# Two matrix products after an attention stage: other token blocks, and W_out decoded at another place

## Chip, cores and metric

One core of one Trainium2 chip. The metric is the device time of one launch in microseconds, lower is better.

## What is computed

A decayed causal attention over 4 x 8 heads of 576 tokens, then two MLP layers on the 2304 rows of width 512 that it gives (hidden width 2048). All in f32.

```python
def _attn_ref(q, k, v, f):                     # q, k, v: 4 x 8 x 576 x 64
    scores = scale * np.matmul(q, k.transpose(0, 1, 3, 2))
    cum = np.cumsum(np.log(np.clip(f, 0.0001, 1.0)), axis=-1)
    scores = np.where(causal, -1e9, scores + cum[:, :, :, None] - cum[:, :, None, :])
    attn = np.exp(scores - np.max(scores, axis=-1, keepdims=True))
    return np.matmul(attn / (np.sum(attn, axis=-1, keepdims=True) + 1e-09), v)
...
x = attn_out.transpose(0, 2, 1, 3).reshape(2304, 512)
h = x @ w_in;  x = np.maximum(0.01 * h, h) @ w_out          # layer 1: w_in 512 x 2048
h = x @ w_in2; x = (h / (1.0 + np.exp(-h))) @ w_out2        # layer 2
```

## The kernel before

**Engines and precision.** TensorE (PE) does all products. An f32 product is three matmuls of rounded parts (high x high, high x low, low x high), so that each operand is first split by a cast on ScalarE (ACT) and a subtraction on VectorE (DVE). The weights come in a wide format and are decoded (`to_f32`: one ACT and three DVE instructions for 128 x 512 values).

**Attention.** Each of the 4 sequences is worked in two halves, queries 0 to 255 and 256 to 575: 8 half-sequences (`sb`) of 8 heads, 64 heads in all, numbered in the order in which they run. A head of an even `sb` gives 256 tokens, one of an odd `sb` 320. Per head: scores on PE (tile `sps`), mask and row minimum on DVE (L688), exp and scaling on ACT and DVE (`sc`), transposes on PE (`tps`), and for each pair of heads the product with v (`av`). `to_ring` splits its result into the tiles `ring`, the input of layer 1.

**Layer 1.** `CHUNKS` (L52) cuts the 2304 tokens into six blocks of 256, 320, 512, 512, 384 and 320. The first product (`hidden`) runs block by block; in each, 16 slices of the hidden width with 12 matmuls, 192 in all (`hps` in the first block, `hpw` in the others). A block can start as soon as all heads that give its tokens are done (`x_ready`); until attention ends it fills PE between the steps of attention. Even blocks lie in the tiles `ring0`, odd ones in `ring1`; `to_ring` waits for a tile until the block two places before it is done. `gate` applies the leaky ReLU (ACT) and stores the result in DRAM (`g1_d`). After attention the second product (`first_values`, `summed`) reads it back in the same six blocks: `gl` loaded through four tiles `ring0`, each with two slices, split into `gs`, and 192 matmuls per block into `acc`. `finish` stores the result (`x1_d`).

**Weights.** `conv_in` decodes W_in. `conv_out` decodes W_out (ACT and DVE, tiles `wst`, `ct`, `wy`) and puts it in DRAM (`wo_d`), 16 slices; `out_weights` fetches it again (`wz`) when the last block of the first product gives its slots back. During the second product `second_weights` decodes and combines the weights of layer 2 on DVE (`f`), spills them (`w2_d`, L1680) and fetches them (`ws`).

**Layer 2.** Seven products in place of eight (`m`, L1333 and L1472), in blocks of 384 columns, then 256. The banks of PSUM alternate between two sets, block by block.

**What sets the order.** The program is written by a planner (`Plan`) that gives every operation a cost, a rank and the names that it waits for, and issues the lowest rank that is ready on each engine; its times decide nothing but the order. On the chip each engine and the DMA queue SP run their list strictly in that order and wait where data is missing.

Of the kernel before, what the change touches and what calls it, by code (L numbers as in the profile page):

```python
# [21 lines left out]
GT_BUFS = 3  # L22
RING_BUFS = 4
WST_BUFS = 2
WY_BUFS = 3
Z_BUFS = 2
U_BUFS = 2
# [21 lines left out]
EDGES = [[0, 128, 256], [0, 107, 214, 320, 448, 576]]  # L49

TURNS = [[[(0, 1)]], [[(0,), (1,)], [(2,), (3, 4)]]]
CHUNKS = ((0, 256), (256, 320), (576, 512), (1088, 512), (1600, 384), (1984, 320))  # L52
SET_A = ("sp", "sp", "sp", "av")
SET_B = ("h", "h", ("acc", 0), ("acc", 1))

# [203 lines left out]
def fused_kernel(ctx, tc, qt, kt, va, vb, ft, w1, wi2, wo2, out):  # L259
# [6 lines left out]
    T = 256  # L266
    TW = 512
    NCH = len(CHUNKS)
    NST = FF // 2
    NP = FF // 2  # L270
    NSB = 2 * B
# [16 lines left out]
    cum_d = dram.tile([H * B, 4, S], F32, name="cum_d")  # L288
    cum_p = dram.tile([H * B, 2, S], F32, name="cum_p")
    wo_d = dram.tile([FF, 128, DM], F32, name="wo_d")  # L290
    g1_d = dram.tile([NCH, NST, 128, 2, TW], F32, name="g1_d")
    x1_d = dram.tile([NG, 128, KC, 2 * TB], F32, name="x1_d")
    g2_d = dram.tile([NG, 4, 128, 4, 2, TB], F32, name="g2_d")
    w2_d = dram.tile([2, 128, 2 * NU, 256], F32, name="w2_d")
# [708 lines left out]
        signal("hidden")  # L1003

    def gate(j, s):
        n = CHUNKS[j][1]
        i_g = yield take("g", G_BUFS)
        if (j, s) == (NCH - 1, NST - 1):
            signal("gated")
        g = main.tile([128, 2, n], F32, tag="g", name="gw", bufs=G_BUFS)  # L1010
        if j == 0:
            hp_t, held = hp.pop((j, 2 * s))
            yield act(2 * n, lambda: nc.scalar.activation(g, hp_t, ACTF.Prelu, alpha=0.01), 1, 0.05)
            give(*held)
        else:
            for part in range(2):
                yield wait(("hp", j, 2 * s + part))
                hp_t, held = hp.pop((j, 2 * s + part))
                yield act(n, lambda: nc.scalar.activation(g[:, part], hp_t, ACTF.Prelu, alpha=0.01), 1, 0.05)
                give(*held)  # L1020
        yield dma(1024 * n, lambda: nc.sync.dma_start(out=g1_d[j, s, :, :, 0:n], in_=g))
        give("g", i_g)
        signal(("g1", j, s))
        if (j, s) == (NCH - 1, NST - 1):
            one = stats[0][0:1, 0:1]
            yield op("act", 1.4, lambda: nc.scalar.activation(one, one, ACTF.Silu), 0)
# [23 lines left out]

    def first_values():

        yield wait(("ring_free", NCH - 2))

        def split(j, s, n, cuts, src, i):
            flat = src.rearrange("p a t -> p (a t)")
            for parts in cuts:
                cols = len(parts) * n
                part = flat[:, parts[0] * n:(parts[-1] + 1) * n]
                i_g = yield take("g", G_BUFS)  # L1060
                t = main.tile([128, 2, cols], F32R, tag="g", name="gs", bufs=G_BUFS)
                yield act(cols, lambda: nc.scalar.copy(t[:, 0], part), 0, 0.09)  # L1062
                yield less(cols, t[:, 1], part, f32(t[:, 0]), "d", 0, PE_LAT)
                for k, a in enumerate(parts):
                    gs[j, 2 * s + a] = t[:, :, k * n:(k + 1) * n], i_g if k == len(parts) - 1 else None
                    signal(("gs", j, 2 * s + a))
            give("ring0", i)

        def splits():
            yield wait("gated")  # L1070
            for j, (_, n) in enumerate(CHUNKS):
                for s in range(NST):
                    yield wait(("gl", j, s))
                    yield from split(j, s, n, ((0, 1),) if j == 0 else ((0,), (1,)), *loaded.pop((j, s)))
            signal("g_last")

        loaded = {}
        p.start(splits())
        for j, (_, n) in enumerate(CHUNKS):
            for s in range(NST):  # L1080
                yield wait(("g1", j, s))
                i = yield take("ring0", RING_BUFS)
                src = main.tile([128, 2, n], F32, tag="ring0", name="gl", bufs=RING_BUFS)
                yield dma(1024 * n, lambda: nc.sync.dma_start(out=src, in_=g1_d[j, s, :, :, 0:n]), 0)
                loaded[j, s] = src, i
                signal(("gl", j, s))

    def summed():
        for j, (_, n) in enumerate(CHUNKS):
            yield wait("hidden" if j else "attention")  # L1090
            acc, held = [], []
            for name in (SET_A, SET_B)[j % 2]:
                t, h = yield from bank(name, [128, n], "acc")
                acc.append(t)
                held.append(h)
            signal(("set", j))
            for f in range(FF):
                yield wait(("gs", j, f), ("woh", f))
                w, i_w = wo_h[f]
                g, i_g = gs.pop((j, f))  # L1100

                def product(c):
                    for r, (wi, gi) in enumerate(((0, 0), (0, 1), (1, 0))):
                        nc.tensor.matmul(  # L1104
                            acc[c], w[:, wi, c * 128:(c + 1) * 128], g[:, gi],
                            start=(f == 0 and r == 0), stop=(f == FF - 1 and r == 2), skip_group_check=True,
                        )

                for c in range(KC):
                    yield op("pe", mm_cost(n, 3), lambda: product(c), 1, 0)  # L1110
                if i_g is not None:
                    give("g", i_g)
                if j == NCH - 1:
                    give(("w", ROOM_W[f]), i_w)
            p.start(finish(j, acc, held))
        signal("summed")

    def finish(j, acc, held):
        o, n = CHUNKS[j]

        def one(c):
            i = yield take("gtmp", GT_BUFS)
# [51 lines left out]
    def second_input():  # L1174
        yield wait("attention")
        for g in range(NG):
            yield wait(*[("x1", j) for j, (o, n) in enumerate(CHUNKS) if o < 2 * TB * (g + 1) and o + n > 2 * TB * g])
            if g:
                yield wait(("m", NP * g - STAGE_LEAD[g - 1], 7))
            i_f = yield take("f", F_BUFS)  # L1180
# [54 lines left out]

    def acc_set():

        k = sets_n[0] % 2
        sets_n[0] += 1
        names = [("sp", 3)] * 3 + [("av", 1)] if k == 0 else [("h", 2)] * 2 + [(("acc", a), 1) for a in range(2)]  # L1240
        held, banks = [], []
        for name, bufs in names:
# [51 lines left out]
    def order2():  # L1294
        items = []
        for n, (g, j) in enumerate(pairs):
            turn = TURN_FIRST[n] if n < 2 else TURN_LAST if n == len(pairs) - 1 else TURN
            items += [(7 * n + pos, n, g, j, q) for q, pos in turn]
        return sorted(items)

    def bank2(n, role):

        name, bufs = ((("sp", 3), ("sp", 3), ("av", 1)), (("h", 2), (("acc", 1), 1), ("h", 2)))[n % 2][role]
        i = yield take(name, bufs)
        pool_, tag = (ps_h, "h") if name == "h" else (ps_acc, f"acc{name[1]}") if name[0] == "acc" else (ps_at, name)
        return pool_.tile([128, TB], F32, tag=tag, name="m", bufs=bufs), (name, i)
# [1 line left out]
    def hidden2():  # L1308
        yield wait("attention")
        held = {}  # L1310
        for _, n, g, j, q in order2():
            if q == 1:
                if n < 2:
                    yield wait(("set", NCH - 2 + n))
                held[n] = [(yield from bank2(n, 0)), None, None]
                p.start(gate2(n, g, j, held[n]))
            if q == 5:
# [274 lines left out]
    def first_weights():  # L1592
# [206 lines left out]
```

## Time and profile before

| | us |
|---|---|
| median of 3 runs | 979.99 (979.06 to 984.43) |
| profiled execution | 978.69 |
| its span | 977.0 |
| PE busy | 961.0 (98%) |
| DVE busy | 678.2 (69%) |
| ACT busy | 573.3 (59%) |

Attention lasts to about 360 us, the first product to 407 us, the second to 617 us, then come the two products of layer 2. A matmul is recorded from its start to the modelled end, and neighbours overlap; what one costs is the distance between starts, so the length of a run divided by its count.

### The profile page before, as it was taken

Reading aid. Unit: us, or ns where it says so; the run is one execution under the profiler, and the core shown is the slowest. Engines: PE = TensorE matmul, PEld = TensorE weight load, DVE = VectorE, ACT = ScalarE, POOL = GpSimd, SP = SyncE. Lnnn points to the kernel's source line nnn. Section 1 sums busy time; section 2 is a strip of 40 time slices with the busy share of each in tenths; the row PEclk is TensorE's granted clock in tenths of the full one; section 3 lists DMA queues with packets and bytes.
Section 4 is the critical chain, followed back from the end, with each engine's and each line's share of the span. In section 5 each row is a group of like instructions: output and inputs, shape, how many; then the busy total and the mean of one; then the engine's idle time right before and its main releaser. Section 6 shows DMA issues by size and latency. Waiting matters only on the chain.

```text
span 977.0 us, 17674 instructions
## 1 busy us (share of the span) xinstructions
PE 961.0 (98%) x6241; PEld 874.6 (90%) x6241; DVE 678.2 (69%) x1673; ACT 573.3 (59%) x1285; POOL 62.6 (6%) x79
## 2 busy tenths in 40 slices
PE   9999999999999999999999999999999999999998
PEld 8787987787677889998788899999999999999998
DVE  6998899798678620478777885434144489998884
ACT  7988898877577633634333444546456665454442
POOL 2001221122112000000000000000000020000000
PEclk9999999999899999999999999999999999999999
DMA  8933676785164215789979878552267764554442
GB/s 234 293 105 122 210 237 204 235 276 167 52 205 143 93 65 172 239 309 330 339 278 344 275 278 252 185 196 101 97 203 220 234 216 131 151 152 132 129 129 65
DMA packets 135252, 190.47 MB, mean 195 GB/s; under 512 B 9958, under 2 KB 105854, under 8 KB 135132
## 3 DMA queue, kind: packets, MB, share of 16 engines
q1 hardware_dynamic: 134732, 188.95, 59.7%
q8 instruction: 49, 0.80, 0.3%
q10 hardware_dynamic: 432, 0.39, 0.1%
q14 instruction: 39, 0.32, 0.1%
HBM read 122.79 MB, written 66.50 MB: 194 GB/s over the span
## 4 chain that ended last, share of the span: by engine, by line
PE 82%; DVE 9%; DMA 4%; ACT 3%; issue 2%; SPq 0%; DVEq 0%; ACTq 0%
PE m L1333 18%; PE m L1472 17%; PE hpw L926 16%; PE acc L1104 13%; PE sps L708 6%; PE av L857 5%; PE tps L789 5%; DMA wst<-in_wi_dram 1%; PE hps L926 1%; DMA wz<-wo_d 1%; PE fps L429 1%; DVE gs L337 1%; DVE sc L688 1%; DMA wst<-in_wo_dram 1%; DVE xa L337 1%
## 5 line engine op out<-in xcount | busy, mean ns | idle before, releaser
L926 PE MATMUL hpw<-ring,w 128*128 128x320 f32 (+2 forms) x960 | 207.3, 353 | 0.3 <-DVE ring L337 0.2
L1104 PE MATMUL acc<-gs,wo 128*128 128x320 f32 (+3 forms) x1152 | 202.6, 336 | 3.6 <-ACT gs L1062 2.1
L1104 PEld LDWEIGHTS acc<-gs,wo 128*128 128x128 f32 x1152 | 185.1, 188 | 20.5 <-DVE gs L337 2.8
L926 PEld LDWEIGHTS hpw<-ring,w 128*128 128x128 f32 x960 | 157.1, 189 | 10.3 <-DVE ring L337 0.9
L1333 PE MATMUL m<-xa,w 128*128 128x384 f32 x576 | 113.5, 339 | 0.6 <-ACT m L1359 0.6
L1472 PE MATMUL m<-w,xa 128*128 128x256 f32 x924 | 113.2, 280 | 0.7 <-DVE xa L337 0.6
L1472 PEld LDWEIGHTS m<-w,xa 128*128 128x128 f32 x924 | 110.6, 188 | 1.4 <-DVE xa L337 1.3
L731 ACT ACTIVATE sc<-sc,st 128x576 f32<-128x576 f32 (+4 forms) x160 | 93.1, 582 | 28.8 <-DVE st L688 27.2
L1333 PEld LDWEIGHTS m<-xa,w 128*128 128x128 f32 x576 | 101.9, 188 | 1.1 <-ACT m L1359 0.9
L1062 ACT CAST gs<-gl 128x512 fp32r<-128x512 f32 (+2 forms) x88 | 47.3, 543 | 84.3 <-PE acc L1104 75.2
L688 DVE CUSTOM_DVE_ANT_0 sc<-sps,zmask 128x288 f32<-128x288 f32 (+4 forms) x160 | 71.3, 449 | 27.7 <-PE sps L708 19.6
L1333 PE MATMUL m<-xb,w 128*128 128x384 f32 x432 | 86.3, 336 | 0.3 <-ACT z L1373 0.3
L322 ACT CAST xa<-g 128x512 fp32r<-128x512 f32 x88 | 49.6, 568 | 48.5 <-PE m L1472 26.0
L1333 PEld LDWEIGHTS m<-xb,w 128*128 128x128 f32 x432 | 76.0, 188 | 0.8 <-ACT z L1373 0.7
L1472 PE MATMUL m<-w,xb 128*128 128x256 f32 x588 | 74.2, 283 | 0.3 <-DVE xb L337 0.3
L789 PE MATMUL tps<-ident,sc 66*107 66x66 f32 (+3 forms) x480 | 68.8, 273 | 5.0 <-ACT sc L741 1.9
L1472 PEld LDWEIGHTS m<-w,xb 128*128 128x128 f32 x588 | 72.0, 191 | 0.7 <-DVE xb L337 0.7
L789 PEld LDWEIGHTS tps<-ident,sc 66*107 66x107 f32 (+3 forms) x480 | 56.0, 152 | 17.5 <-ACT sc L741 3.4
L337 DVE TENSOR_TENSOR gs<-gl,gs 128x512 fp32r<-128x512 f32 (+2 forms) x88 | 51.7, 591 | 28.3 <-ACT gs L1062 28.0
L333 POOL TENSOR_TENSOR m<-qk,m 64x288 fp32r<-64x288 f32 (+1 forms) x58 | 51.9, 905 | 262.9 <-ACT m L322 161.9
L708 PE MATMUL sps<-m,s 66*128 66x288 f32 (+9 forms) x288 | 66.6, 315 | 0.3 <-ACT pf L322 0.2
L1171 DVE TENSOR_TENSOR g<-g 128x256 f32<-128x256 f32 x144 | 61.4, 429 | 6.9 <-DMA g<-g_d 5.9
(129 smaller groups left out, 1313.5 us busy)
## 6 DMA issues: line engine op xcount, KB each, us to landing
g_d<-z SPq DMA_DIRECT2D x24, 768.0 KB
g<-g_d SPq DMA_DIRECT2D x36, 512.0 KB
w_d<-f SPq DMA_DIRECT2D x16, 896.0 KB
ws<-w_d SPq DMA_DIRECT2D x56, 256.0 KB
wst<-in_w_dram SPq DMA_DIRECT2D x17, 512.0 KB
g_d<-gw SPq DMA_DIRECT2D x16, 512.0 KB
wst<-in_wi_dram SPq DMA_DIRECT2D x16, 512.0 KB
gl<-g_d SPq DMA_DIRECT2D x16, 512.0 KB
```

The costliest lines, as they stand in the source:

```text
L322: ("act", act_cost(n, base), lambda: nc.scalar.copy(dst, src), 0.0),
L333: nc.gpsimd.tensor_tensor(dst[:, s_], a[:, s_], b[:, s_], op=ALU.subtract)
L337: ("dve", dve_cost(n), lambda: nc.vector.tensor_tensor(dst, a, b, op=ALU.subtract), 0.0),
L688: yield dve(w, lambda: nc.vector.tensor_tensor_reduce(out=sc[0:qn, k0:k0 + w], in0=ps[0:qn], in1=zmask[0:qn, z0:z0 + w], scale=-0.125, sca ...
L708: nc.tensor.matmul(ps[0:qn], ht[x][:, qs], ht[y][:, k0:k0 + w], start=r == 0, stop=r == len(ops) - 1)
L731: yield act(kn, lambda: nc.scalar.activation(sc[0:qn, 0:kn], sc[0:qn, 0:kn], ACTF.Exp, scale=-1.0, bias=st[0:qn, 2 * i + a:2 * i + a + 1], ...
L789: nc.tensor.transpose(ps[0:k1 - k0, o:o + qn], ht["p"][i][0:qn, k0:k1], ident[0:qn, 0:qn])
L926: nc.tensor.matmul(dst, w[:, wi, c * 128:(c + 1) * 128], x(xi, c), start=(first_ and c == 0 and r == 0), stop=(c == KC - 1 and r == 2), sk ...
L1104: nc.tensor.matmul(acc[c], w[:, wi, c * 128:(c + 1) * 128], g[:, gi], start=(f == 0 and r == 0), stop=(f == FF - 1 and r == 2), skip_group ...
L1171: ("dve", dve_cost(n), lambda: nc.vector.tensor_tensor(dst, a, b, op=op_), 0.0),
L1333: nc.tensor.matmul(dst, w[:, wi, c * 128:(c + 1) * 128], x[:, xi, c], start=start and c == 0 and r == 0, stop=stop and c == 1 and r == 2, ...
L1472: nc.tensor.matmul(banks[b][:, e], t[:, gi, a * 128:(a + 1) * 128], w[:, wi], start=begin and a == 0 and r == 0, stop=jp == NP // 2 - 1 an ...
```

## The change

`CHUNKS` now has eight blocks, 256 and 320 in turn, so that each is exactly one half-sequence of attention. The second product has blocks of its own, `SUMS`: 256 and four of 512. `g1_d` is laid out by token, and a load of the second product waits for the blocks that cover it. The second product has five blocks and not six, so that the sets of banks in layer 2 are swapped (`NCS`), and the two special orders at the start of layer 2 (`TURN_FIRST`) are gone. `conv_out` waits until head 40 has its first scores (`OUT_AT`).

```diff
+OUT_AT = 40
-CHUNKS = ((0, 256), (256, 320), (576, 512), (1088, 512), (1600, 384), (1984, 320))
+CHUNKS = ((0, 256), (256, 320), (576, 256), (832, 320), (1152, 256), (1408, 320), (1728, 256), (1984, 320))
+SUMS = ((0, 256), (256, 512), (768, 512), (1280, 512), (1792, 512))
...
-    g1_d = dram.tile([NCH, NST, 128, 2, TW], F32, name="g1_d")
+    g1_d = dram.tile([NST, 128, 2, NT], F32, name="g1_d")
...
-        yield dma(1024 * n, lambda: nc.sync.dma_start(out=g1_d[j, s, :, :, 0:n], in_=g))
+        yield dma(1024 * n, lambda: nc.sync.dma_start(out=g1_d[s, :, :, o:o + n], in_=g))
...
-        for j, (_, n) in enumerate(CHUNKS):
+        for j, (o, n) in enumerate(SUMS):
             for s in range(NST):
-                yield wait(("g1", j, s))
+                yield wait(*[("g1", k, s) for k, (o1, n1) in enumerate(CHUNKS) if o1 < o + n and o1 + n1 > o])
...
-            turn = TURN_FIRST[n] if n < 2 else TURN_LAST if n == len(pairs) - 1 else TURN
+            turn = TURN_LAST if n == len(pairs) - 1 else TURN
...
-        k = sets_n[0] % 2
+        k = (sets_n[0] + NCS) % 2
         sets_n[0] += 1
+        if sets_n[0] == 2:
+            yield wait(("m", len(pairs) - 1, 5))
...
         yield par(fetches(), *[line(conv_in, ins) for _ in range(C_LINES)])
+        yield wait(("scored", OUT_AT, 0))
         yield par(*[line(conv_out, outs) for _ in range(WST_BUFS)])
```

**PE at the start of head 48** (the first of the seventh half-sequence). `sps` are its scores, `tps` the transposes of heads 46 to 48, `av` a product with v, `hpw` the first product. Before:

```order
L926 MATMUL hpw<-ring,w 128x512 x3
L708 MATMUL sps<-m_3601,s_3603 128x256
L708 MATMUL sps<-m_3602,s_3604 128x256
L789 MATMUL tps<-ident,sc 107x66
L789 MATMUL tps<-ident,sc 107x128 x2
...
L789 MATMUL tps<-ident,sc 128x128 x6
L708 MATMUL sps<-m_3658,s_3660 128x128
L708 MATMUL sps<-m_3659,s_3661 128x128
L857 MATMUL av<-pf,v_3594 64x320 x6
```

and now:

```order
L929 MATMUL hpw<-ring,w 128x256 x3
L711 MATMUL sps<-m_3564,s_3566 128x256
L711 MATMUL sps<-m_3565,s_3567 128x256
L929 MATMUL hpw<-ring,w 128x256 x21
L792 MATMUL tps<-ident,sc 107x66
L792 MATMUL tps<-ident,sc 107x128 x2
...
L929 MATMUL hpw<-ring,w 128x256 x9
L792 MATMUL tps<-ident,sc 106x66
L792 MATMUL tps<-ident,sc 106x128 x2
L792 MATMUL tps<-ident,sc 128x128 x3
L929 MATMUL hpw<-ring,w 128x256 x3
```

Before, no `hpw` stands between the scores of head 48 and those of head 49 and 50; now 21 stand ahead of the first transpose and 15 more ahead of the scores of head 49, the last three behind a transpose that the rows no longer show.

**SP early in the second product.** `gl` is the input of the second product, `w_d` the spill of the weights of layer 2, which waits for DVE, `ws` and `wst` are fetched weights, `x_d` is the result of a block. Before:

```order
L1084 DMA gl<-g_d 128x2x320
L1680 DMA w_d<-f 128x1792
L1699 DMA ws<-w_d 128x512 x2
L1650 DMA wst<-in_wi_dram 128x1024
L1084 DMA gl<-g_d 128x2x320
```

and now:

```order
L1087 DMA gl<-g_d 128x2x512
L1135 DMA x_d<-ev 128x256 x3
L1686 DMA w_d<-f 128x1792
L1656 DMA wst<-in_wi_dram 128x1024
L1087 DMA gl<-g_d 128x2x512
```

A load still stands behind a spill; each load now carries 512 tokens and not 320.

**SP late in attention** (heads 58 to 63). `qk`, `s`, `m` and `v` are inputs of heads, `g_d` the stores of `gate`, `wo_d` those of the decoded W_out. Before:

```order
L632 DMA qk<-in_kt_dram 128x576
L640 DMA qk<-in_qt_dram 128x320
L646 DMA s_4459<-cum_d 2x320
L602 DMA v_4474<-in_vb_dram 128x2x320
L647 DMA m_4457<-cum_d 2x576
L1021 DMA g_d<-gw 128x1024
```

and now:

```order
L635 DMA qk<-in_kt_dram 128x576
L643 DMA qk<-in_qt_dram 128x320
L649 DMA s_4857<-cum_d 2x320
L1024 DMA g_d<-gw 256x1x320
L1593 DMA wo_d<-wy 128x512
L650 DMA m_4855<-cum_d 2x576
```

The 16 stores of `wo_d` stood among the loads of heads up to the middle of attention; now they stand among those of the last third.

## Rows read from the trace of the kernel before

**Rows 1.** Page: PE total, clock in 40 slices, both products (count | busy, mean ns).
```profile
PE 961.0 (98%) x6241; PEld 874.6 (90%) x6241; DVE 678.2 (69%) x1673; ACT 573.3 (59%) x1285; POOL 62.6 (6%) x79
...
PEclk9999999999899999999999999999999999999999
...
L926 PE MATMUL hpw<-ring,w 128*128 128x320 f32 (+2 forms) x960 | 207.3, 353 | 0.3 <-DVE ring L337 0.2
L1104 PE MATMUL acc<-gs,wo 128*128 128x320 f32 (+3 forms) x1152 | 202.6, 336 | 3.6 <-ACT gs L1062 2.1
```

**Rows 2.** Timeline of PE, 360 to 625 us: start, length, count, [idle before <-releaser].
```profile
359.77 47.73 PE L926 MATMUL hpw<-ring,w 128*128 128x384 f32 x304
407.33 6.03 PE L1104 MATMUL acc<-gs,wo 128*128 128x256 f32 x49
...
453.15 0.41 PE L1104 MATMUL acc<-gs,wo 128*128 128x320 f32 x1 [1.05 <-ACT gs L1062]
453.84 18.36 PE L1104 MATMUL acc<-gs,wo 128*128 128x320 f32 x95 [0.28 <-DVE gs L337]
473.24 0.50 PE L1104 MATMUL acc<-gs,wo 128*128 128x512 f32 x1 [1.04 <-ACT gs L1062]
474.14 84.79 PE L1104 MATMUL acc<-gs,wo 128*128 128x512 f32 x384 [0.39 <-DVE gs L337]
...
593.47 23.92 PE L1104 MATMUL acc<-gs,wo 128*128 128x320 f32 x162
617.23 1.22 PE L1333 MATMUL m<-xa,w 128*128 128x384 f32 x6
```

**Rows 3.** Windows, all engines: length, busy (count) PE PEld DVE ACT POOL, clock, DMA.
```profile
125.00:150.00 25.00, 24.32 (x178) 22.08 (x177) 23.00 (x72) 23.39 (x59) 5.44 (x6) 1.00 0.72 230
225.00:250.00 25.00, 24.81 (x149) 19.98 (x148) 20.59 (x65) 17.83 (x48) 7.03 (x7) 1.00 0.39 130
250.00:275.00 25.00, 22.51 (x131) 15.93 (x130) 14.71 (x55) 14.96 (x46) 2.99 (x5) 0.86 0.23 74
300.00:325.00 25.00, 25.00 (x152) 20.30 (x153) 20.35 (x64) 19.09 (x46) 4.25 (x5) 1.00 0.34 112
480.00:540.00 60.00, 60.00 (x266) 49.69 (x265) 46.47 (x88) 22.74 (x38) 0.00 (x0) 1.00 0.87 317
```

**Rows 4.** Timeline of PE around the start of head 48, columns as in Rows 2.
```profile
250.76 2.49 PE L857 MATMUL av<-pf,v 107*64 107x320 f32 x20
...
257.08 0.90 PE L926 MATMUL hpw<-ring,w 128*128 128x512 f32 x3
...
258.97 0.50 PE L789 MATMUL tps<-ident,sc 66*107 66x66 f32 x2 [0.75 <-ACT sc L741]
...
261.97 1.54 PE L789 MATMUL tps<-ident,sc 128*128 128x128 f32 x6 [1.38 <-DVE pf L323]
...
264.20 4.59 PE L857 MATMUL av<-pf,v 107*64 107x320 f32 x20
```

**Rows 5.** Tile wy: ns min/median/max, first and last start, of decoding W_out.
```profile
L1517 ACT ACTIVATE wy<-wst x16: 653/670/682, 94.7 to 223.3; 128x512 f32<-128x512 f32 x16
L1518 DVE TENSOR_SCALAR ct<-wy x16: 395/422/428, 95.5 to 224.0; 128x512 int32<-128x512 int32 x16
L1519 DVE SCALAR_TENSOR_TENSOR ct<-wy,ct x16: 671/688/694, 95.9 to 226.2; 128x512 int32<-128x512 int32 x16
L1521 DVE SCALAR_TENSOR_TENSOR wy<-wst,ct x16: 672/682/692, 97.6 to 227.8; 128x512 int32<-128x512 int32 x16
```

**Rows 6.** Timeline of the SP queue in the second product, columns as in Rows 2.
```profile
438.66 0.52 SPq L1084 DMA_DIRECT2D gl<-g_d  x1
443.33 0.33 SPq L1680 DMA_DIRECT2D w_d<-f  x1
...
446.78 0.52 SPq L1084 DMA_DIRECT2D gl<-g_d  x1
```

**Rows 7.** Waits of the SP queue, 90 to 240 us: total, times, longest.
```profile
SPq L1588 <- DVE wy L1521: 10.8, 5, 4.0
```

More of the change, by code (lines that the diff above doesn't have):

```diff
@@ L268, in fused_kernel @@
     NCH = len(CHUNKS)
+    NCS = len(SUMS)
     NST = FF // 2
@@ L1005, in gate @@
     def gate(j, s):
-        n = CHUNKS[j][1]
+        o, n = CHUNKS[j]
         i_g = yield take("g", G_BUFS)
@@ L1051, in first_values @@
     def first_values():
-        yield wait(("ring_free", NCH - 2))
+        yield wait(("ring_free", max(j for j in range(NCH) if j % 2 == 0)))
         def split(j, s, n, cuts, src, i):
@@ L1070, in splits @@
             yield wait("gated")
-            for j, (_, n) in enumerate(CHUNKS):
+            for j, (_, n) in enumerate(SUMS):
                 for s in range(NST):
                     yield wait(("gl", j, s))
-                    yield from split(j, s, n, ((0, 1),) if j == 0 else ((0,), (1,)), *loaded.pop((j, s)))
+                    yield from split(j, s, n, ((0, 1),) if n <= T else ((0,), (1,)), *loaded.pop((j, s)))
             signal("g_last")
@@ L1078, in first_values @@
         p.start(splits())
-        for j, (_, n) in enumerate(CHUNKS):
+        for j, (o, n) in enumerate(SUMS):
             for s in range(NST):
-                yield wait(("g1", j, s))
+                yield wait(*[("g1", k, s) for k, (o1, n1) in enumerate(CHUNKS) if o1 < o + n and o1 + n1 > o])
                 i = yield take("ring0", RING_BUFS)
                 src = main.tile([128, 2, n], F32, tag="ring0", name="gl", bufs=RING_BUFS)
-                yield dma(1024 * n, lambda: nc.sync.dma_start(out=src, in_=g1_d[j, s, :, :, 0:n]), 0)
+                yield dma(1024 * n, lambda: nc.sync.dma_start(out=src, in_=g1_d[s, :, :, o:o + n]), 0)
                 loaded[j, s] = src, i
@@ L1088, in summed @@
     def summed():
-        for j, (_, n) in enumerate(CHUNKS):
+        for j, (_, n) in enumerate(SUMS):
             yield wait("hidden" if j else "attention")
@@ L1112, in summed @@
                     give("g", i_g)
-                if j == NCH - 1:
+                if j == NCS - 1:
                     give(("w", ROOM_W[f]), i_w)
@@ L1118, in finish @@
     def finish(j, acc, held):
-        o, n = CHUNKS[j]
+        o, n = SUMS[j]
         def one(c):
@@ L1176, in second_input @@
         for g in range(NG):
-            yield wait(*[("x1", j) for j, (o, n) in enumerate(CHUNKS) if o < 2 * TB * (g + 1) and o + n > 2 * TB * g])
+            yield wait(*[("x1", j) for j, (o, n) in enumerate(SUMS) if o < 2 * TB * (g + 1) and o + n > 2 * TB * g])
             if g:
@@ L1301, in bank2 @@
     def bank2(n, role):
-        name, bufs = ((("sp", 3), ("sp", 3), ("av", 1)), (("h", 2), (("acc", 1), 1), ("h", 2)))[n % 2][role]
+        name, bufs = ((("sp", 3), ("sp", 3), ("av", 1)), (("h", 2), (("acc", 1), 1), ("h", 2)))[(n + NCS) % 2][role]
         i = yield take(name, bufs)
@@ L1313, in hidden2 @@
                 if n < 2:
-                    yield wait(("set", NCH - 2 + n))
+                    yield wait(("set", NCS - 2 + n))
                 held[n] = [(yield from bank2(n, 0)), None, None]
```

## The prediction

> **What bounds the kernel now.** I read the page first: PE is busy for 961.0 of the 977.0 us of the span [rows 1], so only two things can move the time: how much work PE has, and the few places where it stands still or runs slowly. The reader is to see in the clock line of the page that one slice of 40 is not at full clock, and nothing else is.
>
> Then I read what one matmul costs, from runs without a gap on PE's timeline [rows 2, 3]. 320 columns: 162 matmuls from 593.47 to the next start at 617.23 us, which is 23.76 / 162 = 146.7 ns. 512 columns: 266 in 60 us, 225.6 ns. 256 columns: 49 in 6.03 us, 123 ns at most, since that length holds the tail of the last one. 384 columns: the run of 304 from 359.77 to 407.33 us holds 112 of them and 192 of 320; 47.56 - 192 x 0.1467 = 19.4 us, 173 ns. At 2.4 GHz the columns alone take 133.3, 213.3, 106.7 and 160 ns. So every matmul pays some 13 ns (12.3 to 16) whatever its width, and the rest is columns, which this change leaves alone.
>
> Third, the windows and timelines of the two places at which PE loses time.
>
> *Start of head 48, 258 to 269 us* [rows 3, 4]. The window of 250 to 275 us has 22.51 us of busy PE, against 24.81 in the one ahead and 25.00 in that of 300 to 325, and a granted clock of 0.86. The timeline shows why: behind the last product at 257.08 and the scores of head 48 no product of layer 1 is left to run, and the transposes wait 0.75 us for ACT and 1.38 us for DVE. Then the 20 matmuls of `av`, which took 2.49 us at 250.76, take 4.59 us at 264.20: PE is on its lower level of 1.2 GHz. The cause is in the blocks: the third one (576 to 1087) ends here, and the fourth (1088 to 1599) needs all tokens to 1599, the last of which come from heads 40 to 47, which are only being finished.
>
> *Second product, 446 to 474 us* [rows 2, 6]. PE waits 1.05, 0.28, 1.04 and 0.39 us for split inputs, 2.76 us together. The SP queue issued a load of `gl` at 438.66 and the next at 446.78, 8.1 us later: between them stands the spill at 443.33, which waited for DVE.
>
> **The change part by part.**
>
> *More and fewer matmuls.* A block has 192 matmuls whatever its width. The first product goes from six blocks (960 + 192) to eight (1536), the second from six (1152 [rows 1]) to five (960). That is 192 more at 13 ns: **+2.5 us** on PE, with nothing to hide it, since PE is the bound. From the ends of the fixed cost it is 2.3 to 3.1.
>
> On this the Trainium skill speaks against the change: "TensorE: Matmul & The Clock Gate", section "Back-to-back issue gap", gives sustained spacings of about 81 ns for 128 columns and 131 ns for 512, by which narrow matmuls are much dearer per column than wide ones; drawn as a straight line that is an estimate of 98, 106 and 114 ns for 256, 320 and 384, by which the two products together would grow by some 12 us and the sum come to 983. The trace does not agree: 512 columns take 225.6 ns [rows 3], which is the columns and a small rest, and the measurement decides.
>
> *The gap at head 48.* Now each block is one half-sequence, so at head 48 the blocks of earlier half-sequences are whole and ready. The order shows it: where no matmul of layer 1 stood between the scores of heads 48 and 49, 36 of 256 columns stand now, 36 x 0.12 = 4.3 us of work, the first 21 (2.5 us) ahead of the first transpose. The waits there were 2.1 us together [rows 4], so they are covered. What goes is the idle time over that of a usual window, 2.49 - 0.19 = 2.3 us, and the cycles of the low clock, 0.14 x 25 = 3.5 us [rows 3]: **-5.8 us**. What is late next is nothing on this trace: in 300 to 325 us, with 512-wide filler at hand, PE has no idle time at all. If the attention steps still come late, less of it goes; the least is nothing.
>
> *The longer hold of `ring1`.* Blocks of 320 all lie in `ring1`, so a head pair of half-sequence 5 waits for the block of half-sequence 3. The order shows 72 matmuls of the first product in a row at head 46 because of it. PE works meanwhile, so this costs nothing by itself; behind it attention has the next block of 256 as cover.
>
> *W_out decoded later.* Nothing is added: 16 slices of 0.42 + 0.69 + 0.68 = 1.79 us on DVE and 0.67 us on ACT [rows 5], 28.6 and 10.7 us in all. They ran from 95 to 228 us and now run from head 40 to the end of attention, some 135 us as well. That is 5.3 us of DVE and 2.0 of ACT per 25 us. Without it DVE and ACT have 20.35 and 19.09 us in 300 to 325; with it, 25.7 and 21.1, so DVE alone would be over the brim, though some copies and scalings may go to either engine, and the sum of 46.7 is that of 125 to 150 us today (23.00 + 23.39 = 46.4), where PE is idle 0.68 us in 25 [rows 3]. Over 135 us this price is 5.4 x 0.68 = 3.7 us; the first half of attention, freed of the same load, can give the same back. The range is -3.7 to +3.7 and I take **0**. Behind the 16 stores stand loads of heads on SP; today SP waits 10.8 us for DVE at five of them [rows 7], and PE's windows there lose little.
>
> *Second product in 512s.* Four buffers of `gl` hold two slices each. One of 320 feeds PE for 24 x 0.1467 = 3.5 us, one of 512 for 24 x 0.2256 = 5.4 us. With three in hand that is 10.6 us against 16.2. The hole in the queue was 8.1 us, and PE's first wait ended at 453.15, up to 6.4 us behind the issue at 446.78 [rows 2, 6]; 14.5 us together, more than 10.6 and less than 16.2. So most of the 2.76 us should go; a fuller DMA queue could keep it. Range 0 to -2.8; I take **-2.0**.
>
> *Order at the start of layer 2, swapped banks, layout of `g1_d`.* The same bytes and the same instructions. Between the last `acc` and the next seed matmul (L1357) stand 18 matmuls now and six before; I take 0, and -0.5 to +1 for the range.
>
> Sum against the profiled execution: 978.7 + 2.5 - 5.8 + 0 - 2.0 + 0 = **973.4 us**. The profiled execution is 1.3 us under the median of 979.99; I make no correction for it.
>
> **The rivals.**
>
> *The gap only moves.* Attention may be held by its own chain, and the filler that is used up early may be missing elsewhere, at head 32 or 62 for example. Then only the added matmuls stay: 978.7 + 2.5 = **981.2 us**. For it: the same filler is spread over the same attention work. Against it: PE is hardly ever idle but at this place [rows 3], and the low clock comes from this place alone [rows 1].
>
> *DVE becomes the bound of late attention* (the slower side). From head 40 on the decode of W_out raises DVE to 25.7 us per 25 us in half-sequences of 320 tokens; the stores on SP wait for it, and the loads of the next heads behind them. Each of heads 40, 48 and 56 would then begin as head 48 does today, three gaps of 5.8 us in place of one, with the second product unchanged: 978.7 + 2.5 - 5.8 + 3 x 5.8 = **992.8 us**. It decides from the point where DVE has under 5.3 us of room in 25; it has 4.65 in 300 to 325 [rows 3], while ACT has 5.91 and can take part of the load. Against it: 125 to 150 us today has the same sum of DVE and ACT and loses 0.68 us.
>
> *Narrow matmuls are dearer than the fixed 13 ns,* because the load of the weights no longer hides behind them. A load takes 49.69 / 265 = 188 ns [rows 3]; if a matmul of 256 columns had to last as long, 576 more of them would cost 65 ns each, 37 us: 978.7 + 2.5 + 37 - 5.8 - 2.0 = **1010.4 us**. Against it stands that those of today, with the same loads, start every 123 ns [rows 2]. (Dearer narrow matmuls are also what the section of the Trainium skill named above gives.)
>
> *More is given back.* The early half of attention, without the decode, loses less (3.7), and the second product keeps no wait (2.8): 978.7 + 2.5 - 5.8 - 3.7 - 2.8 = **968.9 us**.
>
> **How the numbers follow.** About half a per cent, 4.9 us, is what a measurement of this kernel can tell from no change, so that faster means under 975.1 and slower over 984.9. The forecast and its near neighbours (969 to 978) have a chance of 0.52, of which 0.43 lies under 975.1; more given back 0.16; the gap that only moves 0.18; DVE as the bound 0.13; dearer narrow matmuls 0.01. Faster is 0.43 + 0.16 = 0.59, the same 0.09 + 0.18 = 0.27, slower 0.13 + 0.01 = 0.14. The range goes from 967.5, just under the best case, to 984, over the case at 981.2 with a second product that waits 2.8 us more; it leaves out the two slower cases and a little below.
>
> **What would show it.** A granted clock of 1.00 in every window and no idle PE around head 48 show the gap closed; idle PE of over a microsecond at another head shows it moved. 1536 and 960 matmuls at unchanged spacings show the 2.5 us. Waits of over 0.5 us for split inputs in the second product would show the -2.0 wrong. PE waiting for DVE behind head 40, with DVE at 24 us or more in 25, would show the slower rival. The prediction is wrong if attention, and not PE, sets the pace of heads 40 to 63.

## The result

The changed kernel takes **969.69 us** (median of 4 runs, 968.12 to 970.4), the kernel before 980.11 beside it (979.06 to 984.43): a ratio of **0.9881 [0.9853, 0.9909]**. Taken again later on a chip beside the others, it was 968.85 us and 0.9883 [0.9857, 0.9909]. The profiled execution took 969.07 us, with a span of 967.3 us.

So it is faster, as forecast, and inside the range; but of the profiled time 9.6 us went and not 5.3, so that 4.3 us of gain were not foreseen.

The page of the changed kernel, the lines that answer to [rows 1], in the same columns:

```profile
PE 955.8 (99%) x6433; PEld 878.2 (91%) x6433; DVE 669.3 (69%) x1645; ACT 573.7 (59%) x1296; POOL 56.1 (6%) x73
...
PEclk9999999999999999999999999999999999999999
...
L929 PE MATMUL hpw<-ring,w 128*128 128x320 f32 (+1 forms) x1344 | 216.0, 303 | 0.1
L1107 PE MATMUL acc<-gs,wo 128*128 128x512 f32 (+1 forms) x960 | 199.0, 369 | 0.7 <-ACT gs L1065 0.4
```

Busy PE fell from 961.0 to 955.8 us though it has 192 matmuls more; the one slice with a low clock is gone; and the second product's idle time in front of its matmuls fell from 3.6 to 0.7 us. ACT is busy as long as before, and DVE 8.9 us less.

The windows that answer to [rows 3], with one more of the second product (columns as there):

```profile
125.00:150.00 25.00, 24.96 (x183) 22.75 (x182) 21.79 (x68) 21.78 (x57) 5.79 (x6) 1.00 0.45 140
225.00:250.00 25.00, 23.94 (x173) 22.03 (x171) 18.66 (x53) 18.00 (x45) 3.51 (x4) 1.00 0.58 192
250.00:275.00 25.00, 24.54 (x202) 21.57 (x201) 16.46 (x57) 16.73 (x50) 1.57 (x3) 1.00 0.62 193
300.00:325.00 25.00, 24.59 (x177) 21.69 (x175) 24.06 (x76) 22.52 (x58) 4.05 (x5) 1.00 0.66 223
450.00:475.00 25.00, 25.00 (x112) 20.69 (x111) 19.77 (x38) 9.71 (x16) 0.00 (x0) 1.00 0.90 322
```

At 250 to 275 us, where head 48 starts, the clock is 1.00 and no longer 0.86, and PE does 202 matmuls where it did 131. The decode of W_out now lies in these windows: at 300 to 325 us DVE is up from 20.35 to 24.06 us, and PE is no longer wholly without idle time there (24.59). At 225 to 250 us it has 23.94 us where it had 24.81, in two waits of 0.37 and 0.69 us for ACT and DVE, with the clock at 1.00. The second of the two stands behind the long run of the first product at head 46, which the forecast had named as the longer hold of `ring1`:

```profile
234.80 10.84 PE L929 MATMUL hpw<-ring,w 128*128 128x320 f32 x75
246.33 2.49 PE L860 MATMUL av<-pf,v 107*64 107x320 f32 x20 [0.69 <-DVE ring L340]
```

In the last window PE is full; in the same one of the kernel before it was not:

```profile
450.00:475.00 25.00, 22.21 (x116) 18.77 (x115) 20.42 (x42) 10.49 (x19) 0.00 (x0) 1.00 0.92 334
```

PE's timeline around the start of head 48, which answers to [rows 4]:

```profile
260.72 0.40 PE L711 MATMUL sps<-m,s 128*128 128x256 f32 x2
260.96 2.68 PE L929 MATMUL hpw<-ring,w 128*128 128x256 f32 x21
263.48 1.19 PE L792 MATMUL tps<-ident,sc 66*107 66x66 f32 x6
264.43 1.32 PE L929 MATMUL hpw<-ring,w 128*128 128x256 f32 x9
...
267.52 2.49 PE L860 MATMUL av<-pf,v 107*64 107x320 f32 x20
```

The 21 matmuls of 256 columns stand where the order had them, the transposes follow without a wait, and the 20 matmuls of `av` take 2.49 us, not 4.59. And PE's timeline in the second product, which answers to [rows 2]:

```profile
364.25 40.30 PE L929 MATMUL hpw<-ring,w 128*128 128x256 f32 x291
404.38 5.96 PE L1107 MATMUL acc<-gs,wo 128*128 128x256 f32 x48
410.71 0.39 PE L1107 MATMUL acc<-gs,wo 128*128 128x256 f32 x1 [0.37 <-ACT gs L1065]
411.44 149.37 PE L1107 MATMUL acc<-gs,wo 128*128 128x256 f32 x725 [0.34 <-DVE gs L340]
```

The first row is the end of the first product. After two short waits at the start, 725 matmuls of the second product run with none. The kernel before has six waits for split inputs there, of which [rows 2] shows four.

**A measure by stage.** To see where the rest went, I took for every kernel the distance from each matmul's start to the next one's, less the columns at 2.4 GHz and 13.5 ns, and summed it by stage. That is the time lost to waits and to the low clock together; "matmuls" is the sum of what was subtracted. Heads are told apart by their scores in PE's list. Some 5 us of each span lie outside the two sums. (us)

| | before | after | d1 | d2 | d3 | d4 | e1 | e2 | e3 | f1 |
|---|---|---|---|---|---|---|---|---|---|---|
| heads 0 to 15 | 26.2 | 26.4 | 26.0 | 25.6 | 26.5 | 28.5 | 25.9 | 26.7 | 25.9 | 26.6 |
| heads 16 to 31 | 11.7 | 10.4 | 10.0 | 13.1 | 11.6 | 10.5 | 11.2 | 10.3 | 11.7 | 10.7 |
| heads 32 to 47 | 11.3 | 9.7 | **19.4** | 10.2 | 11.3 | 8.5 | 11.4 | 8.7 | 11.4 | 7.9 |
| heads 48 to 63, rest of first product | 16.4 | 11.0 | 14.6 | 9.0 | 16.7 | 10.7 | 8.6 | 10.9 | 16.1 | 9.8 |
| second product | 5.5 | 1.7 | 7.5 | 1.3 | 1.5 | 7.3 | 4.7 | **42.7** | 2.6 | 8.3 |
| layer 2 | 3.5 | 3.2 | 3.5 | 3.3 | 3.6 | 2.9 | 3.2 | 3.4 | 3.3 | **7.8** |
| lost in all | 74.6 | 62.4 | 80.9 | 62.5 | 71.1 | 68.4 | 64.9 | 102.8 | 71.0 | 71.2 |
| matmuls | 897.6 | 900.2 | 897.6 | 900.2 | 895.0 | 902.8 | 895.0 | 910.6 | 897.6 | 900.2 |
| span | 977.0 | 967.3 | 983.3 | 967.5 | 970.9 | 976.3 | 964.7 | 1018.4 | 973.4 | 976.3 |

Each column is one profiled execution; the letters are the experiments below. Two of them were profiled twice: the rows of the changed kernel came out within 0.1 us of each other (g1), those of e1 within 1.7 us (g2, whose second product loses 3.0 and not 4.7). So a difference of under 2 us between two columns is not shown by the table alone.

### The profile page after: what moved, and what is told of

Read it like the earlier page. It is cut to its first block, busy times and chain, and to the rows that moved or that the text cites. A ratio compares the mean times of both kernels' runs of the same rounds, so it can differ in the third digit from the quotient of the medians.

```text
span 967.3 us, 18030 instructions
## 1 busy us (share of the span) xinstructions
PE 955.8 (99%) x6433; PEld 878.2 (91%) x6433; DVE 669.3 (69%) x1645; ACT 573.7 (59%) x1296; POOL 56.1 (6%) x73
## 4 chain that ended last, share of the span: by engine, by line
PE 77%; DVE 10%; DMA 6%; ACT 5%; issue 2%; SPq 0%; DVEq 0%; ACTq 0%
PE m L1338 18%; PE m L1477 17%; PE acc L1107 17%; PE hpw L929 12%; PE sps L711 4%; PE av L860 4%; PE tps L792 3%; DMA qk<-in_kt_dram 2%; DMA wst<-in_wo_dram 2%; DVE sc L691 2%; ACT sc L734 1%; DMA wst<-in_w_dram 1%; PE hps L929 1%; ACT sc L744 1%; DVE sc L742 1%
## 5 line engine op out<-in xcount | busy, mean ns | idle before, releaser
L929 PE MATMUL hpw<-ring,w 128*128 128x320 f32 (+1 forms) x1344 | 216.0, 303 | 0.1
L1107 PE MATMUL acc<-gs,wo 128*128 128x512 f32 (+1 forms) x960 | 199.0, 369 | 0.7 <-ACT gs L1065 0.4
L1107 PEld LDWEIGHTS acc<-gs,wo 128*128 128x128 f32 x960 | 167.3, 189 | 30.6 <-ACT gs L1065 0.6
L929 PEld LDWEIGHTS hpw<-ring,w 128*128 128x128 f32 x1344 | 189.1, 190 | 2.0 <-issue 1.0
L691 DVE CUSTOM_DVE_ANT_0 sc<-sps,zmask 128x288 f32<-128x288 f32 (+4 forms) x160 | 71.1, 449 | 32.6 <-PE sps L711 23.9
L1065 ACT CAST gs<-gl 128x512 fp32r<-128x512 f32 x72 | 44.6, 621 | 72.2 <-PE acc L1107 66.5
L325 ACT CAST xa<-g 128x512 fp32r<-128x512 f32 x88 | 49.5, 568 | 47.8 <-PE m L1477 22.8
L340 DVE TENSOR_TENSOR gs<-gl,gs 128x512 fp32r<-128x512 f32 x72 | 49.5, 688 | 23.4 <-ACT gs L1065 23.2
L1022 ACT ACTIVATE gw<-hpw 128x320 f32<-128x320 f32 (+1 forms) x112 | 45.1, 410 | 30.9 <-PE hpw L929 27.2
```

The costliest lines, as they stand in the source:

```text
L325: ("act", act_cost(n, base), lambda: nc.scalar.copy(dst, src), 0.0),
L340: ("dve", dve_cost(n), lambda: nc.vector.tensor_tensor(dst, a, b, op=ALU.subtract), 0.0),
L691: yield dve(w, lambda: nc.vector.tensor_tensor_reduce(out=sc[0:qn, k0:k0 + w], in0=ps[0:qn], in1=zmask[0:qn, z0:z0 + w], scale=-0.125, sca ...
L929: nc.tensor.matmul(dst, w[:, wi, c * 128:(c + 1) * 128], x(xi, c), start=(first_ and c == 0 and r == 0), stop=(c == KC - 1 and r == 2), sk ...
L1107: nc.tensor.matmul(acc[c], w[:, wi, c * 128:(c + 1) * 128], g[:, gi], start=(f == 0 and r == 0), stop=(f == FF - 1 and r == 2), skip_group ...
```

## The experiments

Two parts of the gain were taken from the forecast: filler at head 48, since the first product is cut where half-sequences end, and wide slices in the second product. The theory on the 4.3 us that were not foreseen was that the late decode brings most of them, since it frees the first half of attention. The rival: the place of the decode is worth nothing in all, as forecast, and the other two parts are larger than they were put.

### d1: the decode alone, late

Against the kernel before:

```diff
+        yield wait(("scored", 40, 0))
         yield par(*[line(conv_out, outs) for _ in range(WST_BUFS)])
```

> The kernel before with one edit: W_out is decoded from head 40 on. Theory (the gap at head 48 comes from the blocks, and the decode only loads DVE and ACT): the gap of about 6 us at head 48 stays, windows from 100 to 225 us give back some 3 to 4 us, those behind give 1 us away; 977.5 us. Rival (the decode among heads 17 to 45 is what made attention late at head 48): the gap closes here too, 973 us or less. Rival (late decode makes DVE the bound): 985 us or more.

Measured: 982.39 us, 1.0029 [1.0006, 1.0052] of the kernel before. A miss. The lost time at heads 48 to 63 went down (16.4 to 14.6), but that at heads 32 to 47 went up by 8.1 us: by 4.8 in half-sequence 4 (heads 32 to 39), where a gap opens at the start, and by 3.3 in half-sequence 5, where the decode now runs. Windows of this kernel (columns as above), then PE's timeline at the start of head 32:

```profile
150.00:175.00 25.00, 22.20 (x137) 16.23 (x137) 14.14 (x49) 14.49 (x43) 3.26 (x4) 0.95 0.22 65
175.00:200.00 25.00, 24.83 (x141) 18.73 (x138) 15.83 (x64) 17.72 (x56) 4.73 (x6) 0.91 0.54 169
```

```profile
167.78 0.40 PE L708 MATMUL sps<-m,s 128*128 128x256 f32 x2
168.93 0.50 PE L789 MATMUL tps<-ident,sc 66*107 66x66 f32 x2 [0.75 <-ACT sc L741]
169.59 0.95 PE L789 MATMUL tps<-ident,sc 128*107 128x128 f32 x7 [0.16 <-ACT sc L741]
171.76 0.95 PE L789 MATMUL tps<-ident,sc 128*128 128x128 f32 x6 [1.21 <-DVE pf L323]
173.38 0.66 PE L708 MATMUL sps<-m,s 128*128 128x128 f32 x2 [0.68 <-DVE pf L323]
173.97 4.75 PE L857 MATMUL av<-pf,v 107*64 107x320 f32 x20
178.65 1.23 PE L708 MATMUL sps<-m,s 128*128 128x256 f32 x6
179.72 0.39 PE L926 MATMUL hpw<-ring,w 128*128 128x512 f32 x1
```

From 167.8 to 179.7 us no matmul of the first product runs, the transposes wait 0.75, 0.16 and 1.21 us, the scores 0.68, and `av` takes 4.75 us. That is the gap of [rows 4] once more, 16 heads earlier. The one at head 48 stays, smaller: half-sequence 6 loses 7.8 us, against 9.9 before. Both kernels have issued 420 matmuls of the first product when the transposes of head 32 begin; but in the kernel before 411 of them lie ahead of that head's scores and six behind the last of these, as cover, and here 417 lie ahead and none behind. So with six blocks the freed DVE does not pay: the filler is used up sooner, and none is left as cover. (The profiled execution is 2.7 us above the median of its ten, so the trace shows the gap rather too large.)

### d2: all of the change, but the decode early

```diff
-OUT_AT = 40
+OUT_AT = 18
```

> The changed kernel with one edit: W_out is decoded from head 18 on, nearly where it was before. Theory (blocks close the gap, the late decode adds 3 to 4 us of its own): 973 us, with PE at full clock around head 48 and the loss back in the windows of 100 to 225 us. Rival (the move of the decode is worth nothing): 969.7 us. Rival (late decode costs more than it gives): 967 us.

Measured: 969.34 us, 0.9895 [0.9862, 0.9929], the time of the whole change. So the rival was right and the theory fell: the decode's place is worth nothing in all, within intervals of some 3 us each way. In the table, heads 16 to 31 lose 13.1 us with the early decode and 10.4 with the late one; heads 48 to 63 lose 9.0 and 11.0. The load is moved and its price with it. Two windows of this kernel that answer to those of the changed one:

```profile
125.00:150.00 25.00, 23.66 (x171) 20.96 (x170) 23.41 (x66) 21.66 (x54) 6.40 (x7) 1.00 0.69 230
300.00:325.00 25.00, 25.00 (x185) 23.00 (x184) 21.60 (x70) 21.82 (x56) 2.04 (x2) 1.00 0.39 125
```

With the early decode PE has 23.66 us at 125 to 150 and 25.00 at 300 to 325; with the late one 24.96 and 24.59.

### d3 and d4: the two products apart

d3 has the second product of the change, and the first product and the decode of before (the diffs from here on stand against the changed kernel, where nothing else is said):

```diff
-CHUNKS = ((0, 256), (256, 320), (576, 256), (832, 320), (1152, 256), (1408, 320), (1728, 256), (1984, 320))
+CHUNKS = ((0, 256), (256, 320), (576, 512), (1088, 512), (1600, 384), (1984, 320))
...
-        yield wait(("scored", OUT_AT, 0))
```

> The second product in its own five blocks alone; first product in six blocks and decode as before. Theory (192 matmuls fewer at 13 ns, 2.5 us, and the waits of 4.2 us gone because a buffer of 512 tokens feeds PE longer): 973.4 us, no wait for split inputs over 0.5 us. Rival (the waits come from the full DMA queue, whatever the width): 977.6 us.

Measured: 973.08 us, 0.9927 [0.9905, 0.9949].

d4 has the first product and decode of the change, and the second product in the six blocks of before:

```diff
-SUMS = ((0, 256), (256, 512), (768, 512), (1280, 512), (1792, 512))
+SUMS = ((0, 256), (256, 320), (576, 512), (1088, 512), (1600, 384), (1984, 320))
```

> The changed kernel with the second product in the six blocks of before; eight blocks in the first product and late decode stay. Theory (as in the kernel with the second product's blocks alone): 2.5 us for 192 matmuls and 4.2 us of waits come back, 976.2 us. Rival (the waits went because attention and the decode end otherwise): 972.2 us.

Measured: 977.06 us, 0.9965 [0.9944, 0.9986]. Both as the theory had it. The two parts give 0.73% and 0.35%, 1.08% together, against 1.19% of the whole. The windows of d3 at the start of head 48 and in the second product, then the waits of PE in the second product of d4 (total, times, longest):

```profile
250.00:275.00 25.00, 22.38 (x130) 15.66 (x129) 14.34 (x53) 14.77 (x45) 2.90 (x4) 0.86 0.21 61
450.00:475.00 25.00, 25.00 (x112) 20.71 (x111) 20.91 (x41) 9.09 (x15) 0.00 (x0) 1.00 0.90 316
```

```profile
PE acc L1107 <- ACT gs L1065: 2.5, 2, 1.5
PE acc L1107 <- DVE gs L340: 2.1, 5, 0.6
```

d3 keeps the gap at head 48 with its clock of 0.86 and has a full PE in the second product; d4 has the waits there (2.5 + 2.1 us) and, at heads 48 to 63, loses 10.7 us, about as the changed kernel does (11.0). With the same first product ahead of it, the second product loses 1.5 us in wide blocks and 5.5 in the old ones (d3 and the kernel before), or 1.7 and 7.3 (the changed kernel and d4).

### e1: six blocks with another cut

```diff
-CHUNKS = ((0, 256), (256, 320), (576, 256), (832, 320), (1152, 256), (1408, 320), (1728, 256), (1984, 320))
+CHUNKS = ((0, 256), (256, 320), (576, 512), (1088, 320), (1408, 512), (1920, 384))
...
-        yield wait(("scored", OUT_AT, 0))
```

The fourth block ends at token 1407, where half-sequence 4 ends, so it is ready at head 40. Still six blocks, and the decode as before.

> Six blocks again in the first product, 256, 320, 512, 320, 512 and 384 tokens, so that the fourth ends at token 1408, where a half-sequence ends; the second product in its own five blocks; decode of W_out as before. Theory (the gap at head 48 closes as soon as one block of an earlier half-sequence is whole and ready there, and the eight blocks cost 5 us for 384 matmuls): 973.1 less 5.8 is 967.3 us, full clock around head 48. Rival (blocks of one half-sequence each are needed): the gap opens at another head, 973 us. Rival (the longer last block delays the second product): 970 us or more.

Measured: 966.38 us, 0.9844 [0.9824, 0.9864], as the theory had it. A window at the start of head 48, and one at the start of the second product:

```profile
250.00:275.00 25.00, 25.00 (x192) 22.10 (x193) 15.21 (x62) 18.48 (x57) 3.31 (x4) 1.00 0.41 128
400.00:425.00 25.00, 23.29 (x179) 22.89 (x179) 16.14 (x30) 9.20 (x15) 0.00 (x0) 0.93 0.79 269
```

and PE's timeline in that second stretch:

```profile
406.03 0.39 PE L1107 MATMUL acc<-gs,wo 128*128 128x256 f32 x1 [1.37 <-ACT gs L1065]
```

The gap is closed (half-sequence 6 loses 2.4 us, against 4.0 in the changed kernel and 9.9 before) without the 384 more matmuls that eight blocks have in the first product, and without the late decode. What it loses again lies at the start of the second product, in a wait of 1.37 us (0.37 in the changed kernel), with a clock of 0.93 in that window. ACT's timeline shows what stands ahead of that wait: ACT waits 3.38 us for a fetched slice of W_out (`wz`), then loads a table, and only then casts the input for which PE waits:

```profile
403.34 0.62 ACT L325 CAST wo<-wz 128x512 fp32r<-128x512 f32 x1 [3.38 <-DMA wz<-wo_d]
403.98 1.28 ACT L1029 ACT_TABLE_LOAD   x1
405.38 1.12 ACT L1065 CAST gs<-gl 128x512 fp32r<-128x512 f32 x2
```

### e2: narrow blocks in the second product

```diff
-SUMS = ((0, 256), (256, 512), (768, 512), (1280, 512), (1792, 512))
+SUMS = tuple((256 * i, 256) for i in range(9))
```

> The changed kernel with the second product in nine blocks of 256 tokens: 768 more matmuls. Theory (13 ns for each, and four buffers of 256 tokens hold only 11.5 us of PE work, so that the hole in the SP queue comes through): 969.7 + 10 + 4 or more, 983.7 us or more, with waits for split inputs. Rival (fixed cost alone, the waits do not depend on the width): 979.7 us. Rival (narrow matmuls bound by their weight load, 65 ns each): 1020 us.

Measured: 1022.1 us, 1.0419 [1.0394, 1.0444]. The direction was right, the size missed by far. 768 matmuls more are counted with 10.4 us in the measure above; the other 40 us of its profiled execution are lost time. Two windows of it, and the longest waits of the SP queue in and behind the second product:

```profile
500.00:525.00 25.00, 20.22 (x135) 19.20 (x134) 19.34 (x29) 10.94 (x17) 0.00 (x0) 0.86 0.73 250
600.00:625.00 25.00, 25.00 (x211) 25.00 (x210) 6.96 (x11) 6.22 (x11) 0.00 (x0) 1.00 0.35 106
```

```profile
SPq L1686 <- DVE f L1174: 47.2, 12, 6.1
SPq L1135 <- ACT ev L1128: 43.9, 10, 11.7
```

The window at 600 to 625 us is undisturbed: 211 matmuls lie in it, and their starts are 120 ns apart, which is 256 columns (106.7 ns) and 13.3. At 500 to 525 there are 135 in the same time with a clock of 0.86. So the rival at 1020 us, narrow matmuls bound by their weight load, comes within 2 us of the measured time by luck: where nothing else holds PE up, 256 columns cost 120 ns, as in the kernel before. The SP queue, behind which the loads of `gl` stand, waits 47 us for DVE at spills and 44 us for ACT at the stores of `x1_d`.

### e3, f2, f3: the spills on GpSimd's list

```diff
-                yield dma(918e3, lambda: nc.sync.dma_start(
+                yield dma(918e3, lambda: nc.gpsimd.dma_start(
                     out=w2_d[which, :, 7 * j:7 * j + 7],
```

e3 is the kernel before with this edit, f2 is e1 with it, and f3 is e2 with it and with the stores of `x1_d` in `finish` moved in the same way.

> The kernel before with one edit: the spills of the weights of layer 2 are issued by GpSimd, so that they do not stand in the SP list. Theory (the loads of the second product wait behind a spill that waits for DVE): the waits of 4.2 us in the second product go, 976 us. Rival (the DMA queue is full there): the waits stay, 980 us.

> The six other blocks (256, 320, 512, 320, 512, 384) with the spills of layer 2's weights issued by GpSimd. Theory (with blocks of 512 the second product waits for no spill any more; what is left is a gap at its start): no difference, 966.4 us. Rival (the spills still hold loads up): 964 us or less.

> The nine blocks of 256 with the spills and the stores of the second product's results issued by GpSimd. Theory (the loads wait in the SP list behind stores that wait for PE, DVE and ACT): the waits of 42.7 us fall under 10, 985 to 990 us. Rival (four small buffers are too few for the full DMA queue): 1015 us or more.

e3: 977.41 us, 0.9972 [0.9954, 0.999]. The second product loses 2.6 us and no longer 5.5 (the profiled execution, 975.25 us, is the fastest of its ten). The waits of PE for split inputs there, 3.5 us in six before, are now (total, times, longest):

```profile
PE acc L1104 <- DVE gs L337: 0.9, 2, 0.6
PE acc L1104 <- ACT gs L1062: 0.3, 1, 0.3
```

So the spill in SP's list is a part of the waits, with loads of the old width. f2: 969.76 us, 0.9885 [0.9864, 0.9906], no gain over e1: its loads are 512 wide, and its second product loses 5.5 us, 2.6 of them at 490 to 510 us, where e1 loses nothing. f3: 1016.35 us (two runs), 1.0361 [1.0331, 1.0392], a miss: the lost time of the second product falls only from 42.7 to 37.8 us. Rows of f3's SP queue, then PE's timeline behind them:

```profile
486.01 0.52 SPq L1087 DMA_DIRECT2D gl<-g_d  x1
...
495.81 0.90 SPq L1190 DMA_DIRECT2D x1s<-x_d  x2
...
497.85 11.89 SPq L1087 DMA_DIRECT2D gl<-g_d  x5
```

```profile
508.52 3.87 PE L1107 MATMUL acc<-gs,wo 128*128 128x256 f32 x14 [7.76 <-ACT gs L1065]
```

On GpSimd's list the spills come no later than before (the first at 425.5 us, in e2 at 424.0). But SP's list is still held, now at loads for layer 2 (`x1s`, and a fetch of weights in the rows left out): for 11.8 us no load of `gl` is issued, and PE's wait of 7.76 us follows. So f3 does not free the list, and whether nine blocks of 256 fail for the depth of four buffers or for the order of the lists stays open.

The Trainium skill, "DMA: Bandwidth & Descriptors", section "Issuing engines are not separate DMA queues", says that transfers issued on several engines share the same 16 DMA engines, and that this saves only the time a sequencer needs to issue them. e3 differs: to issue the spill of [rows 6] takes 0.33 us, and what the move took away is a wait at the head of an in-order list; the second product lost 2.9 us less.

### f1: the decode later still

```diff
-OUT_AT = 40
+OUT_AT = 56
```

> The changed kernel with one edit: W_out is decoded from head 56 on, in the last eight heads. They last some 55 us, in which DVE has about 10 us of room for the 28.6 us of the decode. Theory (attention's own instructions go first, and some 50 us of nearly idle DVE follow before W_out is needed): 2 to 6 us more, 972 to 976 us. Rival (DVE becomes the bound of attention): the 18 us that don't fit, 988 us. Rival (nothing, DVE does not matter): 969.7 us.

Measured: 979.55 us, 0.9984 [0.9959, 1.0009]: the whole gain is gone, and not where I looked for it. A window in late attention, one at the start of the second product, and PE's longest wait of 250 to 450 us:

```profile
300.00:325.00 25.00, 24.77 (x182) 22.44 (x181) 23.00 (x71) 23.31 (x60) 7.71 (x8) 1.00 0.60 203
400.00:425.00 25.00, 20.45 (x150) 19.62 (x150) 14.04 (x22) 14.95 (x26) 0.00 (x0) 0.93 0.79 252
```

```profile
PE acc L1107 <- ACT gs L1065: 4.0, 1, 4.0
```

DVE is at 23.00 us and PE at 24.77: attention keeps its pace. But the last decoded slice is started at 396.2 us and not at 346.0; behind its first 48 matmuls the second product then waits 4.0 us, in a window in which PE is busy for 20.45 us at a clock of 0.93. The wait is one for W_out: its fetch (`wz`) starts at 397.9 us and not at 378.1, and ACT, whose cast of `gl` PE waits for, stands still ahead of that cast until a fetched slice lands (ACT's waits for it at 385 to 425 us: total, times, longest):

```profile
ACT wo L325 <- DMA wz<-wo_d: 8.1, 5, 4.0
```

Layer 2 loses 7.8 us as well, with a wait of 2.1 us for DVE among it.

### g1, g2: the changed kernel and e1 side by side

No edit: g1 is the changed kernel, g2 is e1.

> The changed kernel as it is, side by side on one chip with the one with six other blocks. Theory (192 matmuls fewer than the kernel before, 384 fewer than the changed one in the first product, but a gap of some 3 us at the start of the second product): 969 to 970 us here, some 3 us more than the other. Rival (both the same): under 1 us between the two ratios.

> Six other blocks (256, 320, 512, 320, 512, 384), decode early, five blocks in the second product, side by side with the changed kernel. Theory: 966 to 967 us. Rival: 969 to 970 us like the changed kernel.

Measured: 968.85 us, 0.9883 [0.9857, 0.9909], and 966.78 us, 0.987 [0.9838, 0.9901]. e1 has the lower ratio both times (0.9844 and 0.987, against 0.9881 and 0.9883), but the intervals overlap, so these runs don't separate the two. By the traces it has 5.2 us less of matmuls and 2.6 us more of lost time, which fits its spans of 964.7 and 964.0 us against 967.3 and 967.4.

## Why the prediction was right, and where its size was not

- **More matmuls, +2.5.** Right. The timeline of the changed kernel has a run of 291 from 364.25 to 404.38 us, 99 of 256 columns and 192 of 320: 40.13 us less 36.16 for the columns is 13.6 ns for each, so 192 more cost 2.6 us. Narrow matmuls are no dearer than that: at 600 to 625 us of e2 the weight loads are busy for all of the window, and still 256 columns start every 120 ns. The straight line drawn through the figures of the Trainium skill, "TensorE: Matmul & The Clock Gate", section "Back-to-back issue gap", gave an estimate of 98 ns there, and the trace does not agree with it at this width either. The rival at 1010 is out.
- **The gap at head 48, -5.8.** Right: half-sequence 6 loses 4.0 and no longer 9.9 us, which is -5.9. d3 keeps the old cut and has 10.1 us and the low clock; e1 has another cut and 2.4. So the cause, no whole block at hand at head 48, is shown, and also that eight blocks are only one way to it.
- **The longer hold of `ring1`, 0.** Nearly right: the run at head 46 is there, and one wait of 0.69 us behind it is all that the trace shows of a price.
- **W_out decoded later, 0.** Right as a total (d2 against the whole change), and by the way that was given: between d2 and the changed kernel, heads 16 to 31 win 2.8 us and the part from head 48 on loses 2.0. Not foreseen was that alone, with the old blocks, it makes the kernel slower, by opening a second gap at head 32 (4.8 us) and by 3.3 us behind head 40 (d1), so that something of the rivals "the gap only moves" and "DVE becomes the bound" is true of this part by itself; and that what limits lateness is not DVE in attention but the second product that needs W_out (f1). The rival in which DVE becomes the bound did not come, though its sign is half there: DVE is at 24.06 us at 300 to 325, just over the 24 that I had named, but PE is busy for 24.59 us there. The sign of a moved gap, more than a microsecond of idle PE at another head, is met at 225 to 250 only by two waits taken together, and the clock stays at 1.00.
- **Second product in 512s, -2.0.** The mechanism was right, its size was not: -3.8 us (5.5 to 1.7). The term was taken from the idle time that the timeline names at four waits, 2.76 us, and a part of it was kept back. By starts these four cost 4.2 us, and all of it went; the rest of the 5.5 lies at two other waits, and the 1.7 that are left lie at the start of the product and near its end. Step by step the working holds: d4 brings the waits back with the old widths, e3 shows the spill as a cause of about half of the loss, e2 shows that 256 wide slices wait far more, though not by what alone.
- **Where the decode hid a part of the gain.** Heads 16 to 47 lose 2.9 us less than before (11.7 to 10.4 and 11.3 to 9.7), which was in no term. d2, with the early decode, has none of that (23.3 us against 23.0 before), but at heads 48 to 63 it wins 7.4 us (16.4 to 9.0), more than the 5.8 of the sum; and e1 against d3, which differ in the cut of the first product alone, wins 8.1 us there (16.7 to 8.6). So the term for the gap was too small by some 2 us. Most of what the new cut wins lies in half-sequence 6 itself (6.4 us in d2, 7.7 in e1), and the late decode, set against d2, moves a part of the gain from the heads behind 48 to those ahead of it. Why the cut wins more there than the idle time and the low clock of the old gap was not tested.
- **Start of layer 2, 0.** It is -0.3, within the spread of the table.

Before and after, then: +2.6 of matmuls, -5.4 at heads 48 to 63 (-5.9 in half-sequence 6, and 0.5 given back in the last), -3.8, -2.9, -0.3, and +0.1 at the start: -9.7 us, the difference of the spans (9.6 by the profiled times). What lies beyond the forecast, 4.4 us by this sum, are the 1.8 of the second product and the 2.9 of heads 16 to 47, less 0.3 by which the other terms differ; by d2 the 2.9 belong to the new cut, and only their place to the decode. The rival "more is given back" (968.9) came closest to the profiled 969.07, in part by luck: it had the second product's waits go, rightly, but took its other 3.7 us from the early half of attention without the decode, and d2 gives the same time with the decode back there.

## What to carry to other kernels

Where a bound engine lives on filler work, cut the filler where its producers end, and look at every boundary: with the old cut, freeing another engine opened a second hole at an earlier boundary (d1), and the right cut in six blocks did as well as eight (e1). Where loads stand in one in-order list with stores that wait for a compute engine, size a load so that what is buffered outlasts the longest hold of that list (512 tokens did here, 320 did not). And take a term of lost time from the distance between starts, not from the waits that a timeline names: here the four waits of [rows 2] cost 4.2 us by the one and 2.76 by the other.

## What was not expected of the hardware

- A pause can be paid twice. In d1 some 2.8 us of waits between 168 and 174 us are followed by an `av` of 4.75 us in place of 2.49, and by a window with a granted clock of 0.91 (175 to 200 us); in e2 the second product waits 12.9 + 9.9 = 22.8 us by name and loses 42.7, with windows at 0.86.
- Matmuls of 256 columns start every 120 ns while each weight load is recorded with 192 ns (e2, 600 to 625 us): the recorded loads overlap one another, and loads that are busy for 25.00 of 25 us were no bound.
- Moving waiting stores to another issuing engine gave 2.9 us in one kernel (e3), nothing in a second (f2), and in a third (f3) 4.9 of 42.7 us, with SP's list still held by other transfers.
